# Attention products in a lent bank, k^T v joined to a q run, and where batch 2's k and v are loaded

## The chip, the cores and the metric

The kernel runs on one core of a Trainium2 chip. The metric is the time of one execution on the device, in microseconds (us), as the median of several runs. One further execution is taken with the hardware profiler; its trace gives the start and duration of every instruction. The engines are named as in the profile: PE (TensorE, its weight loads apart as PEld), DVE (VectorE), ACT (ScalarE), POOL (GpSimd) and SP (SyncE, which issues DMAs). POOL and ACT issue DMAs too. PSUM is the memory that PE writes, in eight banks of 512 float32 columns on 128 partitions; ACT and DVE read it.

## The reference

Eight batches of eight heads, 576 rows, head dimension 64. For each head a 64x64 product of k and v, then q times that product, a root-mean-square normalisation, and the result goes, with heads side by side, into a gated feed-forward layer.

```python
kv = np.einsum('bhsd,bhse->bhde', k, v)
out = np.einsum('bhsd,bhde->bhse', q, kv)
rms = np.sqrt(np.mean(out * out, axis=-1, keepdims=True) + 1e-06)
attn = out / rms * g_norm
x = attn.transpose(0, 2, 1, 3).reshape(4608, 512)
gate = 1.0 / (1.0 + np.exp(-(x @ w_gate)))      # 512 -> 1536
val = x @ w_val
result = (gate * val) @ w_out                   # 1536 -> 512
```

All data are float32 (the weights arrive as float64 and are converted on the chip). Batches are counted from 0 here, as in the code.

## The kernel before, in words

**Chunks.** The 4608 rows are nine chunks of 512. Chunk 0 is computed directly: `plain` (matmuls at L599) for the first layer, L833 for the second. Its matmuls are 128x128 by 512 columns. While it runs, DVE and ACT convert the weights in steps (`convert_step`, CV in the list of places), and POOL forms sums of weights (`w1_sums`, steps W0 and W1). Chunks 1 to 8 use a scheme with fewer products and more sums: 26 products for each of three column groups j in the first layer (`PRODUCTS1`, matmuls at L957, 78 places p = 26 j + i) and 26 in the second (`PRODUCTS2`, L1059). What is done with a product's result stands as text behind it: `o5=A` is a copy by ACT (L923), `o1=o1+B` a sum by DVE (L927), `s2` a sigmoid by ACT (L916), `o5*o1` a product by POOL (L919). In chunk 1 sums of weights of the second layer (`w_form`, L1030 and L1032) are made on DVE and POOL at listed places, and stored to DRAM for later chunks.

**Banks.** The products' results lie in five PSUM banks, numbered 0 to 4. `free` is a queue of them: a product that begins a new result takes the oldest free bank, and `give` puts it back at the end once the program has issued its last reader. The remaining three banks are one tile, `at`, for the attention.

**Attention.** Chunk 0's rows all come from batch 0, whose attention is done ahead of it (`attention`, before 33 us) and isn't touched by the change. While chunk c is computed, batch c+1 passes through `feed`; batch 1 passes through during chunk 0, and batch 2 begins there. A batch has two runs m of four heads. Its steps are:

- `load_late(b)`: eight loads of 256 KB of k and v for the first 512 rows (L134, all on SP), and four loads of 64 KB for the other 64 rows (L139, the tile `rest`; on SP for batch 1, on POOL for batch 2, on ACT for later ones). They land in `h_more`, which has other uses between batches.
- `load_q_run(b, m)`: q of four heads, as eight loads of 72 KB in 128-byte pieces (L119) and four of 8 KB, which hold the last 64 columns of two heads a second time (L120). On POOL for batch 1, else on SP.
- `kv_mm`: k^T v of all eight heads, 32 products with 128 rows of contraction (L389), then 8 of 64 rows, the tails (L396), into one `at` tile. Each product writes a 64x64 block.
- `kv_copy`: two ACT copies into `kvq` (L404, L405). The second puts the heads of rows 64 to 127 a second time on rows 0 to 63.
- `turn`: DVE transposes of q into `qTs` (L408, and L410 for the repeated 64 columns).
- `u_mm` (once for each run): q times k^T v, 36 products of 64x64x64 (L439) into an `at` tile. Slots 0 to 15 of the tile are filled by heads g=0 (rows 0 to 63 of `qTs`, bank 0) and g=1 (rows 64 to 127, bank 1) in turn. The last two slots, 16 and 17, both lie in bank 2, and both are computed on rows 0 to 63, the second from the repeated data.
- `u_square` (ACT, L444), sums (DVE, L447), root (ACT, L450), norms (ACT L479, or DVE L455), and `x_turn` (DVE L462, L464, then DMAs on SP).

**Order.** The order on each engine is the program's order, written by hand. For chunk 0 it is the string `places`: a number is the count of plain matmuls issued, and behind it stand the steps put there. KV and C are `kv_mm` and `kv_copy` of batch 1; au to ax1 and bu to bx1 are its runs 0 and 1; LL2 is `load_late(2)`; KV2, ASIDE and D are batch 2's `kv_mm`, a copy of its result to `kv_ahead`, and the later copy from there to `kvq`. Between KV2 and D batch 1 still needs `kvq`. For chunks 1 to 6 it is the string `where` in `feed`: place p of the first layer, and the steps behind it (u0 and u1 are `u_mm` of the two runs, q0 and q1 `u_square`). From chunk 2 on, `kv_mm` and `kv_copy` are put at places 19 and 20 (21 and 22 for batch 3) by the loop at the end of the file. An instruction that waits holds up everything behind it on its engine.

Of the kernel before, what the change touches and what calls it, by code (L numbers as in the profile page):

```python
# [10 lines left out]
FP32 = mybir.dt.float32  # L11
# [9 lines left out]
def kernel(  # L21
# [34 lines left out]
    NRUN = NHP // 2  # L56
    QW = 2 * S + 2 * HD

# [46 lines left out]
    def load_q_run(b, m):  # L105
        if b >= B:
            return
        if b == 1:
            t = h_main[2 - m].rearrange("p s c -> p (s c)")[:, 4 * NT * P - QW:4 * NT * P]
        else:  # L110
            t = sb.tile([P, QW], FP32, tag="q", name="q", bufs=1)
        main = t[:, 0:2 * S].rearrange("p (e j c) -> p e j c", e=2, c=QB)
        more = t[:, 2 * S:QW].rearrange("p (e j c) -> p e j c", e=2, c=QB)
# [11 lines left out]
    def load_late(b):  # L125


        if b >= B:
            return
        mains = {}  # L130
        for n in range(NHP):
            for name, src in (("k", k), ("v", v)):
                mains[n, name] = t = kv_place(len(mains))
                nc.sync.dma_start(out=t.rearrange("p (h c) -> p h c", h=2),  # L134
                                  in_=src[b, 2 * n:2 * n + 2, 0:S4].rearrange("h (p j) d -> p h (j d)", j=NK4))
        rest = kv_place(len(mains))
        for i, src in enumerate((k, v)):
            for r in range(2):
                (nc.sync if b == 1 else nc.gpsimd if b == 2 else nc.scalar).dma_start(out=rest[PH * r:PH * r + PH, GH * i:GH * i + GH].rearrange("p (h d) -> p h d", d=HD),  # L139
                                  in_=src[b, NHP * r:NHP * r + NHP, S4:S].rearrange("h p d -> p h d"))  # L140
        kv_late[b] = mains, rest
# [126 lines left out]

    kvq = const.tile([P, 2, NRUN, 2, HD], FP32, name="kvq")
    kv_ahead = const.tile([P, NRUN, 2, HD], FP32, name="kv_ahead")  # L270
# [19 lines left out]
    def attention(n, at_ps):  # L290

        b, m = divmod(n, NHP)
        d = {}
        kv = kvq[:, 0, m // 2, m % 2]

# [80 lines left out]
    def feed(b):  # L376

        d = {}

        def kv_mm():  # L380

            mains, rest = kv_late[b]
            d["kv"] = ps = at_ps()[:, 0:NRUN, 0:2 * HD].rearrange("p m (e d) -> p m e d", d=HD)
            for m in range(NRUN):
                for e in range(2):
                    for j in range(NK4):
                        for g in range(2):
                            c = slice(NK4 * HD * e + HD * j, NK4 * HD * e + HD * j + HD)
                            nc.tensor.matmul(ps[HD * g:HD * g + HD, m, e], mains[2 * m + g, "k"][:, c],  # L389
                                             mains[2 * m + g, "v"][:, c],  # L390
                                             start=(e == 0 and j == 0), stop=False, skip_group_check=True)
            for e in range(2):
                for m in range(NRUN):
                    for g in range(2):
                        rs, c = slice(PH * m, PH * m + PH), HD * (2 * g + e)
                        nc.tensor.matmul(ps[HD * g:HD * g + HD, m, e], rest[rs, c:c + HD],  # L396
                                         rest[rs, GH + c:GH + c + HD], start=False, stop=True, skip_group_check=True)

        def kv_set_aside():
            nc.scalar.copy(out=kv_ahead, in_=d["kv"])  # L400
            d["kv"] = kv_ahead

        def kv_copy():
            nc.scalar.copy(out=kvq[:, 0], in_=d["kv"])  # L404
            nc.scalar.copy(out=kvq[0:HD, 1], in_=d["kv"][HD:P])  # L405

        def turn(m, e):
            nc.vector.transpose(qTs[:, S * e:S * e + S], q_late[b, m][:, S * e:S * e + S])  # L408
            if e == 1:
                nc.vector.transpose(qTs[0:HD, 2 * S:QW], q_late[b, m][0:HD, 2 * S:QW])  # L410
                if b > 1:
                    load_q_run(b + (m + 1) // NRUN, (m + 1) % NRUN)
                elif m == NRUN - 1:
                    load_q_run(b + 1, 0)

        def heads_run(m):
# [12 lines left out]

            def u_mm():  # L430
                d["u"] = u = at_ps().rearrange("p r c -> p (r c)")[:, 0:2 * S]
                for t in range(NSL + 1):
                    for g in range(2):
                        if t < NSL - 1 or g == 0:
                            head, s_ = (1, NSL - 1) if t == NSL else (g, t)
                            o = HD * place(head, s_)
                            for e in range(2):
                                c = 2 * S + HD * e if t == NSL else S * e + HD * s_
                                nc.tensor.matmul(u[HD * e:HD * e + HD, o:o + HD],  # L439
                                                 qTs[HD * g:HD * g + HD, c:c + HD],  # L440
                                                 kvq[HD * g:HD * g + HD, t == NSL, m, e], start=True, stop=True)

            def u_square():
                nc.scalar.activation(out=sq, in_=d["u"], func=AF.Square)  # L444

# [44 lines left out]

        kv = [kv_mm, kv_copy, kv_set_aside] if b == 2 else [kv_mm, kv_copy]
        t0, t1 = ([lambda m=m, e=e: turn(m, e) for e in range(2)] for m in range(NRUN))
        u0, u1 = heads_run(0), heads_run(1)
        if b == 1:
            return kv, t0 + t1 + u0 + u1, ()
# [4 lines left out]
                   51:x00 52:x01 53:u1 56:q1 57:s10,s11 60:r1 62:n10,n11 63:n12 65:n13 66:n14 68:n15 69:n16""" if b == 2 else """  # L500
                   5:t00 8:t01 28:u0 29:t10 30:q0 33:s00,s01 36:r0 39:t11 41:n00 47:n01 51:x00,x01 54:u1
                   56:q1,s10,s11 61:r1 64:n10 66:n11""" if b == 3 else """
                   3:t00 7:t01 28:u0,t10 30:q0,s00,s01 37:r0 39:t11 47:n00,n01 53:x00,x01 54:u1
                   56:q1,s10,s11 60:r1 61:n10 63:n11"""
# [63 lines left out]
    def at_ps():  # L568
        return psum.tile([P, NAT, 512], FP32, tag="at", name="at")
# [212 lines left out]
    def w1_form(c, j, part, v):  # L782
        if c == 1:
# [12 lines left out]
    batch1, second_batch = feed(1), feed(2)  # L796
    named = {"LL": lambda: load_late(1), "LL2": lambda: load_late(2), "KV": batch1[0][0], "KV2": second_batch[0][0],
             "W0": lambda: w1_sums(0), "W1": lambda: w1_sums(1),
             "ASIDE": second_batch[0][2], "CV": convert_step}
    named.update({"C": batch1[0][1], "D": second_batch[0][1]})  # L800
    for i in range(NRUN):
        named[f"Q{i}"] = lambda i=i: load_q_run(1, i)
        named.update({f"t{i}{e}": batch1[1][2 * i + e] for e in range(2)})
    for i, which in enumerate("ab"):
        for n, step in enumerate(("u", "sq", "s0", "s1", "rt", "rc", "n0", "n1", "n2", "x0", "x1")):
# [326 lines left out]
    for c in range(1, NG):  # L1132
# [4 lines left out]
        if c + 1 < B:  # L1137
            kv, first_, then = second_batch if c == 1 else feed(c + 1)
            for p, step in (list(zip((21, 22) if c == 2 else (19, 20), kv)) if c > 1 else []) + first_:
                at1.setdefault(p, []).append(step)  # L1140
# [9 lines left out]
        if c == 1:  # L1150
            for at_, forms in ((at1, ((28, 9, 0), (30, 10, 0), (34, 12, 0), (52, 11, 1), (53, 22, 0), (57, 14, 0), (58, 8, 1), (61, 19, 0), (64, 16, 1))), (at2, ((1, 13, 0), (3, 23, 0), (4, 25, 1), (9, 15, 0), (10, 24, 0), (10, 20, 0), (11, 17, 0), (12, 18, 0), (13, 21, 0)))):
                for p, n, pool_ in forms:
# [35 lines left out]
```

## Time and profile before

| what | value |
|---|---|
| median of 3 runs | 1002.54 us (1002.2 to 1002.74) |
| the profiled execution | 1003.68 us |
| its span, first to last instruction | 1001.9 us |
| granted PE clock | 1.0 throughout |
| PE busy with ordinary products of the first layer of chunks 1 to 8, L957 | 51% of the chain |
| the second layer of these, L1059 | 27% of the chain |
| plain matmuls of chunk 0, L599 and L833 | 12% of the chain |
| q times k^T v, L439, 14 runs | 2% of the chain |
| k^T v, L389, 7 batches | 1% of the chain |

The span is what lies between the first and the last recorded instruction; the rest of an execution's time lies around it. The chain is the row of work that ended last, followed back from the last instruction: at each step to what released it, or to the instruction before it on its engine. A matmul of the source is two PE instructions in the trace (float32), and its weights are loaded by two PEld instructions. A duration of a matmul is that of one result passing through, longer than the distance between two starts; a run's time is read from the chain, where pieces follow each other.

In the timelines a row is: start in us, length in us, engine, line, operation, output from input, shapes, how many, and in brackets the idle time of that engine before it, with what ended it.

### The profile page before, as it was taken

How to read it: one execution, taken by the hardware profiler on the slowest of the kernel's cores; microseconds unless marked ns; L12 is line 12 of the kernel's file. 1: busy time of each engine (PE TensorE's matmuls, PEld its weight loads, DVE VectorE, ACT ScalarE, POOL GpSimd, SP SyncE). 2: the span in 40 equal slices, each digit the busy share in tenths (PEclk: the TensorE clock that was granted, in tenths of full speed). 3: DMA queues.
4: the chain of work that ended last, by engine and by line, in shares of the span. 5: the costliest groups of instructions: out<-in, count | busy, mean ns of one | idle time of the engine just before them, and what ended most of it. 6: DMA issues, size and time to landing. Idle time of an engine off the chain costs nothing.

```text
span 1001.9 us, 16623 instructions
## 1 busy us (share of the span) xinstructions
PE 993.2 (99%) x5958; PEld 815.9 (81%) x5958; DVE 723.3 (72%) x1199; ACT 342.2 (34%) x606; POOL 617.8 (62%) x991
## 2 busy tenths in 40 slices
PE   8999999999999999999999999999999999999998
PEld 7445447888888888888888888888888888888887
DVE  4889999889757756784677576866587566755672
ACT  4566322652144213530344124421442133213320
POOL 1509997798259633965196708861596349744963
PEclk9999999999999999999999999999999999999999
DMA  9996514764899568746975677756754555444614
GB/s 256 285 263 192 173 42 119 220 220 134 271 294 267 176 183 239 240 158 197 278 220 170 186 218 244 196 171 193 235 198 159 161 176 208 157 148 162 216 50 124
DMA packets 155155, 195.43 MB, mean 195 GB/s; under 512 B 83809, under 2 KB 127841, under 8 KB 155073
## 3 DMA queue, kind: packets, MB, share of 16 engines
q0 software_dynamic: 22128, 114.37, 34.4%
q1 hardware_dynamic: 126864, 78.16, 27.9%
q10 hardware_dynamic: 6080, 1.84, 0.8%
q8 instruction: 47, 0.77, 0.3%
q14 instruction: 36, 0.29, 0.1%
HBM read 160.50 MB, written 25.56 MB: 186 GB/s over the span
## 4 chain that ended last, share of the span: by engine, by line
PE 94%; POOL 2%; DMA 1%; ACT 1%; SPq 1%; issue 1%; DVE 1%; POOLq 0%; ACTq 0%; DVEq 0%
PE mm L957 51%; PE mm L1059 27%; PE mm L599 8%; PE mm L833 4%; PE at L439 2%; PE at L389 1%; DMA v<-in_v_dram 1%; PE at L599 1%; POOL h_more L733 1%; POOL h L733 1%; POOL h L919 0%; POOL w L1030 0%; SPq L93 0%; PE at L396 0%; DVE sg L927 0%
## 5 line engine op out<-in xcount | busy, mean ns | idle before, releaser
L957 PE MATMUL mm<-xs,w 128*128 128x256 f32 x1428 | 331.9, 380 | 0.0
L957 PEld LDWEIGHTS mm<-xs,w 128*128 128x128 f32 x1428 | 270.4, 190 | 37.4 <-DVE sg L927 0.4
L957 PE MATMUL mm<-xT,w 128*128 128x256 f32 x948 | 229.8, 380 | 0.0
L957 PEld LDWEIGHTS mm<-xT,w 128*128 128x128 f32 x948 | 179.5, 190 | 25.0 <-issue 0.2
L780 POOL DMA_DIRECT2D w<-kept x84 | 46.7, 556 | 192.5 <-PE mm L957 188.5
L927 DVE TENSOR_TENSOR sg<-sg,mm 128x512 f32<-128x512 f32 (+1 forms) x176 | 100.8, 600 | 85.0 <-PE mm L957 40.3
L1059 PE MATMUL mm<-w,h 128*128 128x256 f32 x630 | 142.8, 379 | 0.0
L1059 PEld LDWEIGHTS mm<-w,h 128*128 128x128 f32 x630 | 119.7, 190 | 16.3
L919 POOL TENSOR_TENSOR h<-h,sg 128x512 f32<-128x512 f32 x72 | 96.7, 1360 | 56.4 <-DVE h L927 30.4
L923 ACT COPY temps<-mm 128x512 f32<-128x512 f32 (+1 forms) x128 | 66.1, 538 | 186.7 <-PE mm L1059 94.7
L733 POOL TENSOR_TENSOR h<-h 128x128 f32<-128x128 f32 x216 | 113.1, 535 | 16.5 <-DVE h_more L733 13.1
L1059 PE MATMUL mm<-w,h_more 128*128 128x256 f32 x474 | 108.2, 379 | 0.0
L916 ACT ACTIVATE sg<-sg 128x512 f32<-128x512 f32 x96 | 59.7, 630 | 133.6 <-DVE sg L927 133.6
L1059 PEld LDWEIGHTS mm<-w,h_more 128*128 128x128 f32 x474 | 90.1, 190 | 12.2
L923 ACT COPY sg<-mm 128x512 f32<-128x512 f32 (+1 forms) x112 | 56.9, 510 | 86.4 <-PE mm L1059 45.0
L733 POOL TENSOR_TENSOR h_more<-h 128x128 f32<-128x128 f32 x120 | 61.6, 517 | 35.0 <-DVE h L919 30.8
L927 DVE TENSOR_TENSOR temps<-temps,mm 128x512 f32<-128x512 f32 (+1 forms) x96 | 59.4, 619 | 25.7 <-PE mm L1059 16.5
L599 PE MATMUL mm<-xT,w 128*128 128x512 f32 x176 | 77.8, 596 | 0.1
L927 DVE TENSOR_TENSOR temps<-mm,temps 128x512 f32<-128x512 f32 (+1 forms) x64 | 39.8, 622 | 50.7 <-PE mm L1059 24.3
L923 ACT COPY h<-mm 128x512 f32<-128x512 f32 x48 | 28.1, 585 | 138.3 <-PE mm L957 138.3
L927 DVE TENSOR_TENSOR sg<-mm,sg 128x512 f32<-128x512 f32 (+1 forms) x64 | 39.7, 620 | 46.7 <-PE mm L957 24.7
L599 PEld LDWEIGHTS mm<-xT,w 128*128 128x128 f32 x176 | 32.6, 190 | 39.2 <-issue 36.1
(148 smaller groups left out, 1283.6 us busy)
## 6 DMA issues: line engine op xcount, KB each, us to landing
w<-kept POOLq DMA_DIRECT2D x42, 896.0 KB, 5.4
w<-kept POOLq DMA_DIRECT2D x90, 384.0 KB, 4.8
w<-kept POOLq DMA_DIRECT2D x42, 768.0 KB, 5.0
out_dram<-sg SPq DMA_DIRECT2D x119, 64.0 KB, 1.7
h_more<-in_k_dram SPq DMA_DIRECT2D x28, 256.0 KB, 5.5
h_more<-in_v_dram SPq DMA_DIRECT2D x28, 256.0 KB, 6.2
q<-in_q_dram SPq DMA_DIRECT2D x96, 72.0 KB, 5.0
xT<-xTs SPq DMA_DIRECT2D x96, 72.0 KB, 4.6
```

The costliest lines, as they stand in the source:

```text
L389: nc.tensor.matmul(ps[HD * g:HD * g + HD, m, e], mains[2 * m + g, "k"][:, c], mains[2 * m + g, "v"][:, c], start=(e == 0 and j == 0), stop ...
L439: nc.tensor.matmul(u[HD * e:HD * e + HD, o:o + HD], qTs[HD * g:HD * g + HD, c:c + HD], kvq[HD * g:HD * g + HD, t == NSL, m, e], start=True ...
L599: nc.tensor.matmul(self.ps[i], w[("wg", "wv")[i], self.f][:, m, :], xT[self.c][:, m, :], start=(m == 0), stop=(m == NMT - 1), skip_group_c ...
L733: ops.append((eng, lambda v=v, x=x, sign=sign, y=y, eng=eng: eng.tensor_tensor(out=h_form(v, j), in0=h_form(x, j), in1=h_form(y, j), op=op ...
L780: nc.gpsimd.dma_start(out=granule(g)[:, 0:n], in_=kept1[g // NPA % N3, g % NPA][:, 0:n])
L833: nc.tensor.matmul(ps[t], gv[0, f][:, P * t:P * t + P], w["wo", f], start=(f == 0), stop=(f == NFT - 1), skip_group_check=True)
L916: nc.scalar.activation(out=o["o" + step[1]], in_=o["o" + step[1]], func=AF.Sigmoid)
L919: mult.tensor_tensor(out=o[x], in0=o[x], in1=o[y], op=ALU.mult)
L923: nc.scalar.copy(out=o[out_], in_=o[expr])
L927: tt(out=o[out_], in0=o[x], in1=o[y], op=ALU.add if sign == "+" else ALU.subtract)
L957: nc.tensor.matmul(regions[name][1][:, g], ws[:, g], xf[c][wv], start=(new and g == 0), stop=True, skip_group_check=True)
L1059: nc.tensor.matmul(regions[name][1], h_form(hv, j), ws[:, j], start=(used[i] and j == 0), stop=(j == N3 - 1), skip_group_check=True)
```

## The change

Five things are changed.

1. `u_mm` takes a second bank, `lent`: bank 4 for batch 1, else the oldest free one. Slot 17 (the last one of heads g=1) is computed on rows 64 to 127 into the first 64 columns of that bank. `u_square` begins with an ACT copy of these 64 columns into the `at` tile and, past batch 1, gives the bank back. So the repeated columns of q (their loads and their transpose) and the second half of `kvq` go.
2. `kv_mm` is no longer a step by itself. For batch 1 and for batches 3 to 7 it is issued at the start of `u_mm` of the batch's own run 0, right behind it `kv_copy`, then the q products. For batch 2 it is issued at the start of `u_mm` of batch 1's run 1. Its results lie in two banks: run 0's in the `at` tile, run 1's in the lent bank. The tails come first, except in batch 2.
3. `kv_copy` and `kv_set_aside` are two copies of 128 columns, one for each run.
4. The eight 256 KB loads of batch 2's k and v are issued by POOL instead of SP.
5. Places: batch 1's k^T v goes from 20 to 29 (in au), batch 2's stays at 44 with bu, which was at 47; bsq goes from 48 to 47, ASIDE from 44 to 47. In batches 3 to 7 u0 goes from place 28 to 25. In chunk 1 the sum for form 14 of w_out (DVE) goes from place 57 to 55.

```diff
-    QW = 2 * S + 2 * HD
+    QW = 2 * S
...
-                queue.dma_start(out=more[QB * i:QB * i + QB, e], in_=src[:, JR - 2:JR])
...
-                nc.sync.dma_start(out=t.rearrange("p (h c) -> p h c", h=2),
+                (nc.gpsimd if b == 2 else nc.sync).dma_start(out=t.rearrange("p (h c) -> p h c", h=2),
...
-        def kv_mm():
+        def kv_mm(at, lent):
             mains, rest = kv_late[b]
-            d["kv"] = ps = at_ps()[:, 0:NRUN, 0:2 * HD].rearrange("p m (e d) -> p m e d", d=HD)
+            d["kv"] = ps = [t.rearrange("p (e d) -> p e d", d=HD)
+                            for t in (at[:, NAT - 1, 2 * HD:4 * HD], lent[:, HD:3 * HD])]
+            def tails(first):
+                for e in range(2):
+                    for m in range(NRUN):
+                        for g in range(2):
+                            rs, c = slice(PH * m, PH * m + PH), HD * (2 * g + e)
+                            nc.tensor.matmul(ps[m][HD * g:HD * g + HD, e], rest[rs, c:c + HD],
+                                             rest[rs, GH + c:GH + c + HD], start=first and e == 0, stop=not first,
+                                             skip_group_check=True)
+            if b != 2:
+                tails(True)
             for m in range(NRUN):
                 for e in range(2):
                     for j in range(NK4):
                         for g in range(2):
                             c = slice(NK4 * HD * e + HD * j, NK4 * HD * e + HD * j + HD)
...
+                            nc.tensor.matmul(ps[m][HD * g:HD * g + HD, e], mains[2 * m + g, "k"][:, c],
+                                             mains[2 * m + g, "v"][:, c], start=(b == 2 and e == 0 and j == 0),
+                                             stop=(b != 2 and j == NK4 - 1), skip_group_check=True)
+            if b == 2:
+                tails(False)
         def kv_copy():
-            nc.scalar.copy(out=kvq[:, 0], in_=d["kv"])
-            nc.scalar.copy(out=kvq[0:HD, 1], in_=d["kv"][HD:P])
+            for m in range(NRUN):
+                nc.scalar.copy(out=kvq[:, m], in_=d["kv"][m])
...
-                nc.vector.transpose(qTs[0:HD, 2 * S:QW], q_late[b, m][0:HD, 2 * S:QW])
...
-            def u_mm():
-                d["u"] = u = at_ps().rearrange("p r c -> p (r c)")[:, 0:2 * S]
-                for t in range(NSL + 1):
+            def u_mm(first=()):
+                at = at_ps()
+                d["u"] = u = at.rearrange("p r c -> p (r c)")[:, 0:2 * S]
+                i_ = 4 if b == 1 else free.popleft()
+                lent = bank(i_)
+                for step in first:
+                    step(at, lent)
+                for s_ in range(NSL):
                     for g in range(2):
...
+                        o = HD * place(g, s_)
+                        to = lent[:, 0:HD] if s_ == NSL - 1 and g == 1 else u[:, o:o + HD]
+                        for e in range(2):
+                            c = S * e + HD * s_
+                            nc.tensor.matmul(to[HD * e:HD * e + HD], qTs[HD * g:HD * g + HD, c:c + HD],
+                                             kvq[HD * g:HD * g + HD, m, e], start=True, stop=True)
+                d["lent"] = i_, lent[:, 0:HD], u[:, o:o + HD]
             def u_square():
+                i_, lent, to = d["lent"]
+                nc.scalar.copy(out=to, in_=lent)
+                if b > 1:
+                    give(i_)
                 nc.scalar.activation(out=sq, in_=d["u"], func=AF.Square)
...
+        if b == 2:
+            kv = [kv_mm, kv_copy, kv_set_aside]
+        else:
+            u0[0] = lambda u_mm=u0[0]: u_mm((kv_mm, lambda at, lent: kv_copy()))
+            kv = []
...
+    named["bu"] = lambda: batch1[1][2 * NRUN + 11]((second_batch[0][0],))
...
-        18:CV,CV 19:t01 20:KV 22:CV,CV,C 25:CV 26:CV,CV 29:au,LL2 30:CV
+        18:CV,CV 19:t01 22:CV,CV 25:CV 26:CV,CV 29:au,LL2 30:CV
...
-        43:ax1 44:KV2,ASIDE 46:CV,W0 47:bu 48:CV,CV,bsq 50:CV,bs0 52:CV,CV 54:bs1 55:CV,CV,brt,D 57:CV,CV 58:CV 60:CV,brc
+        43:ax1 44:bu 46:CV,W0 47:bsq,ASIDE 48:CV,CV 50:CV,bs0 52:CV,CV 54:bs1 55:CV,CV,brt,D 57:CV,CV 58:CV 60:CV,brc
```

More of the change, by code (lines that the diff above doesn't have):

```diff
@@ L111, in load_q_run @@
             t = sb.tile([P, QW], FP32, tag="q", name="q", bufs=1)
-        main = t[:, 0:2 * S].rearrange("p (e j c) -> p e j c", e=2, c=QB)
-        more = t[:, 2 * S:QW].rearrange("p (e j c) -> p e j c", e=2, c=QB)
+        main = t.rearrange("p (e j c) -> p e j c", e=2, c=QB)
         queue = nc.gpsimd if b == 1 else nc.sync
@@ L266 @@
     g_col = const.tile([P, 1], FP32, name="g_col")
-    kvq = const.tile([P, 2, NRUN, 2, HD], FP32, name="kvq")
+    kvq = const.tile([P, NRUN, 2, HD], FP32, name="kvq")
     kv_ahead = const.tile([P, NRUN, 2, HD], FP32, name="kv_ahead")
@@ L293, in attention @@
         d = {}
-        kv = kvq[:, 0, m // 2, m % 2]
+        kv = kvq[:, m // 2, m % 2]
         def kv_mm():
@@ L388, in kv_mm @@
                             c = slice(NK4 * HD * e + HD * j, NK4 * HD * e + HD * j + HD)
[L389 to L397, printed above, removed]
+                            nc.tensor.matmul(ps[m][HD * g:HD * g + HD, e], mains[2 * m + g, "k"][:, c],
[3 more added lines that the diff above has]
+                tails(False)
         def kv_set_aside():
-            nc.scalar.copy(out=kv_ahead, in_=d["kv"])
-            d["kv"] = kv_ahead
+            for m in range(NRUN):
+                nc.scalar.copy(out=kv_ahead[:, m], in_=d["kv"][m])
+            d["kv"] = [kv_ahead[:, m] for m in range(NRUN)]
         def kv_copy():
-            nc.scalar.copy(out=kvq[:, 0], in_=d["kv"])
-            nc.scalar.copy(out=kvq[0:HD, 1], in_=d["kv"][HD:P])
+            for m in range(NRUN):
+                nc.scalar.copy(out=kvq[:, m], in_=d["kv"][m])
         def turn(m, e):
@@ L428, in by_head @@
                 return t.rearrange("p (n d) -> p n d", d=HD)
-            def u_mm():
-                d["u"] = u = at_ps().rearrange("p r c -> p (r c)")[:, 0:2 * S]
-                for t in range(NSL + 1):
-                    for g in range(2):
[L434 to L441, printed above, removed]
+            def u_mm(first=()):
[6 more added lines that the diff above has]
+                for s_ in range(NSL):
+                    for g in range(2):
+                        o = HD * place(g, s_)
[5 more added lines that the diff above has]
+                d["lent"] = i_, lent[:, 0:HD], u[:, o:o + HD]
             def u_square():
+                i_, lent, to = d["lent"]
+                nc.scalar.copy(out=to, in_=lent)
+                if b > 1:
+                    give(i_)
                 nc.scalar.activation(out=sq, in_=d["u"], func=AF.Square)
@@ L489, in heads_run @@
                     [lambda i=i: x_turn(i) for i in range(NC)])
-        kv = [kv_mm, kv_copy, kv_set_aside] if b == 2 else [kv_mm, kv_copy]
         t0, t1 = ([lambda m=m, e=e: turn(m, e) for e in range(2)] for m in range(NRUN))
         u0, u1 = heads_run(0), heads_run(1)
+        if b == 2:
[3 more added lines that the diff above has]
+            kv = []
         if b == 1:
@@ L500, in feed @@
                    51:x00 52:x01 53:u1 56:q1 57:s10,s11 60:r1 62:n10,n11 63:n12 65:n13 66:n14 68:n15 69:n16""" if b == 2 else """
-                   5:t00 8:t01 28:u0 29:t10 30:q0 33:s00,s01 36:r0 39:t11 41:n00 47:n01 51:x00,x01 54:u1
+                   5:t00 8:t01 25:u0 29:t10 30:q0 33:s00,s01 36:r0 39:t11 41:n00 47:n01 51:x00,x01 54:u1
                    56:q1,s10,s11 61:r1 64:n10 66:n11""" if b == 3 else """
-                   3:t00 7:t01 28:u0,t10 30:q0,s00,s01 37:r0 39:t11 47:n00,n01 53:x00,x01 54:u1
+                   3:t00 7:t01 25:u0 28:t10 30:q0,s00,s01 37:r0 39:t11 47:n00,n01 53:x00,x01 54:u1
                    56:q1,s10,s11 60:r1 61:n10 63:n11"""
@@ L796 @@
     batch1, second_batch = feed(1), feed(2)
-    named = {"LL": lambda: load_late(1), "LL2": lambda: load_late(2), "KV": batch1[0][0], "KV2": second_batch[0][0],
+    named = {"LL": lambda: load_late(1), "LL2": lambda: load_late(2),
              "W0": lambda: w1_sums(0), "W1": lambda: w1_sums(1),
              "ASIDE": second_batch[0][2], "CV": convert_step}
-    named.update({"C": batch1[0][1], "D": second_batch[0][1]})
+    named["bu"] = lambda: batch1[1][2 * NRUN + 11]((second_batch[0][0],))
+    named.update({"D": second_batch[0][1]})
     for i in range(NRUN):
@@ L804 @@
     for i, which in enumerate("ab"):
-        for n, step in enumerate(("u", "sq", "s0", "s1", "rt", "rc", "n0", "n1", "n2", "x0", "x1")):
+        for n, step in list(enumerate(("u", "sq", "s0", "s1", "rt", "rc", "n0", "n1", "n2", "x0", "x1")))[which == "b":]:
             named[which + step] = batch1[1][2 * NRUN + 11 * i + n]
@@ L1138 @@
             kv, first_, then = second_batch if c == 1 else feed(c + 1)
-            for p, step in (list(zip((21, 22) if c == 2 else (19, 20), kv)) if c > 1 else []) + first_:
+            for p, step in first_:
                 at1.setdefault(p, []).append(step)
@@ L1150 @@
         if c == 1:
-            for at_, forms in ((at1, ((28, 9, 0), (30, 10, 0), (34, 12, 0), (52, 11, 1), (53, 22, 0), (57, 14, 0), (58, 8, 1), (61, 19, 0), (64, 16, 1))), (at2, ((1, 13, 0), (3, 23, 0), (4, 25, 1), (9, 15, 0), (10, 24, 0), (10, 20, 0), (11, 17, 0), (12, 18, 0), (13, 21, 0)))):
+            for at_, forms in ((at1, ((28, 9, 0), (30, 10, 0), (34, 12, 0), (52, 11, 1), (53, 22, 0), (55, 14, 0), (58, 8, 1), (61, 19, 0), (64, 16, 1))), (at2, ((1, 13, 0), (3, 23, 0), (4, 25, 1), (9, 15, 0), (10, 24, 0), (10, 20, 0), (11, 17, 0), (12, 18, 0), (13, 21, 0)))):
                 for p, n, pool_ in forms:
```

## The prediction

> **What bounds the kernel now.** I read the page's busy shares and its chain first, then the chain in order of time, then the timelines around the attention steps.
>
> ```profile
> PE 993.2 (99%) x5958; PEld 815.9 (81%) x5958; DVE 723.3 (72%) x1199; ACT 342.2 (34%) x606; POOL 617.8 (62%) x991
> PE 94%; POOL 2%; DMA 1%; ACT 1%; SPq 1%; issue 1%; DVE 1%; POOLq 0%; ACTq 0%; DVEq 0%
> ...
> 475.84 17.27 PE mm L957 x80
> 493.10 2.02 PE at L389 x64
> 495.12 0.39 PE at L396 x16
> 495.51 7.97 PE mm L957 x36
> 503.48 1.31 PE at L439 x72
> 504.79 22.64 PE mm L957 x104
> ```
>
> TensorE is the bound: from 33 us on the chain is one unbroken row of its work, so only TensorE time counts. The last six rows (start, us) are batch 4: k^T v is 64+16 instructions (each product of the source is two), then nine ordinary products, then q times k^T v, 72 instructions. 17.27/80 is 0.216 us an ordinary instruction; 36 of them should take 7.77 but take 7.97. **So a stretch between two small runs costs 0.20 more**: single starts show 0.09 on going into a small run and 0.10 at the first ordinary instruction after it.
>
> Weight loads of one q run (stretches of 0.23 us; third figure PE busy, fourth PEld):
>
> ```profile
> 503.87:504.10 0.23, 0.23 (x29) 0.23 (x24) 1.00 0.00 0
> 504.10:504.33 0.23, 0.23 (x29) 0.23 (x24) 1.00 0.00 0
> 504.33:504.56 0.23, 0.23 (x23) 0.23 (x16) 1.00 0.00 0
> ```
>
> Full stretches touch 24 weight loads, the last one 16. The single starts say why: 64 instructions go in fours, one four each 0.058 us, the last eight in twos at the same pitch. Those are the slots of the last 64 columns, both done on rows 0 to 63.
>
> **What the change does to that path.**
> (A) The last slot of heads g=1 goes to rows 64 to 127 and a lent bank, so the last eight instructions go as two fours, not four twos: 2 x 0.058 = 0.117 us a run, 14 runs: -1.64. Bounds: 0 (fours don't form) to 1.64. I take 1.64: the 64 others already go in fours, with the two row halves in different banks, which the lent bank keeps.
> (B) k^T v moves next to a q run in all seven batches, and one stretch between small runs goes: 7 x 0.20 = 1.4. For batch 2 k^T v ends with the 64-row tails and q follows in the same shape; the 0.09 of a shape change may go too. Bounds 1.4 to 1.5; I take 1.4, the row of the stretch alone. The row behind the rest is L389 to L396, 0.152 between starts where 0.058 is the pitch. The Trainium skill, TensorEngine Tiling (Array Packing), Key Properties, says that changing the tiling mode drains TensorE and changing the tile does not; by it the 0.09 goes in batch 2 and stays in the other six, and (B) would be 1.5. No run shows the tail-to-q step yet.
> (C) A joined q run needs the copies of its own k^T v. They are now one of 128 columns for each run, and the first q product needs the first copy alone. ACT in batch 4:
>
> ```profile
> 495.58 0.37 ACT L404 COPY kvq<-at 128x256 f32<-128x256 f32 x1 [0.94 <-PE at L396]
> ...
> 499.92 0.63 ACT L916 ACTIVATE sg<-sg 128x512 f32<-128x512 f32 x1 [1.96 <-DVE sg L927]
> 501.79 0.58 ACT L923 COPY h<-mm 128x512 f32<-128x512 f32 x1 [1.23 <-PE mm L957]
> ```
>
> The copy starts 0.07 after its matmul and takes between 0.22 (64 columns, L479) and 0.37 (256): about 0.45 to the release. Meanwhile TensorE does run 1's 32 instructions, 64 in 2.02, so 1.0 us. ACT is free: its sigmoid of product 23 ended at 500.55 and product 25 at 500.8. Cost 0; without the cover 0.45 a batch, 2.7 over six. The lent slot waits for the second copy, but 0.93 us of q products stand ahead of it. Tails first costs nothing: the shape changes are as many.
> (D) Lent banks. In batch 1 bank 4 is idle. Later the run takes the oldest free bank, and the next products get banks whose readers are one step younger. The tightest row is batch 7: DVE's last read of the bank (`h<-mm,temps`, 740.62 for 0.68) ends at 741.30; the lent write comes 0.93 after the run's start at 740.88. Margin 0.5; cost 0, at worst 0.3 in that one batch.
> (E) The 14 new ACT copies of 64 columns (0.22 to 0.37) stand ahead of the Square. For most the next user is half a microsecond or more away. Not in the second run of batch 2: there the copy `sg<-mm` behind the Square ends at about 210.5, and TensorE goes onto that bank at 210.83 without waiting. A copy of 0.25 to 0.37 more: 0 to 0.2; I take +0.1.
> (F) The sum for form 14 of w_out goes from place 57 to 55, on DVE:
>
> ```profile
> 210.09 1.41 DVE L447 TENSOR_REDUCE ms<-sqs 128x9 f32<-128x576 f32 x2 [1.28 <-ACT sqs L444]
> 211.42 1.95 DVE L1032 SCALAR_TENSOR_TENSOR w<-w,w 128x768 f32<-128x768 f32 x1
> ...
> 224.91 2.68 DVE L927 TENSOR_TENSOR sg<-sg,mm 128x512 f32<-128x512 f32 x4
> 226.94 1.10 PE L957 MATMUL mm<-xs,w_ring 128*128 128x256 f32 x4 [0.41 <-POOL h L733]
> ```
>
> DVE stood idle 1.28 us ahead of the reduce, then did the sum, and ran late until TensorE stopped at 226.94. The page names POOL, but that product goes onto a bank that DVE's third `sg<-sg,mm` reads until about 226.8. The row costs 0.65 (the four instructions ahead started at 225.50: 0.57; a slow restart 0.08). In the new order the sum fills the idle time. Part of the lateness comes back from ACT's copies and from DVE's 2.29 us `sg<-temps` at 222.51. Between 0.65 gained and 0.3 lost; I take -0.35.
> (G) Batch 2's eight k, v loads leave SP for POOL and now wait for batch 1's k^T v, at place 29 instead of 20:
>
> ```profile
> 53.66 1.25 POOL L139 DMA_DIRECT2D h_more<-in_k_dram  x2 [12.24 <-PE at L396]
> ...
> 76.37 0.74 POOL L751 TENSOR_TENSOR h_more<-w 128x256 f32<-128x256 f32 x1 [20.24 <-PE at L389]
> ```
>
> Run 0 of batch 1's k^T v will end near 60.05 (the q run began at 61.22, less 2.4 for k^T v now ahead of it in the same place, plus 0.5 tails and 1.0). POOL is idle there. Eight issues of 0.62 end at 65.1, and landing takes 5.9 (median of L134): 71. The four small ones wait for the first landing and land near 73. k^T v of batch 2 starts at 75.3 and needs run 0's loads then, run 1's a microsecond later, the small ones at 77.3. Cost 0. POOL's w1 sums stand behind these loads but start only at 76.37, after that k^T v, as before. On SP nothing gains: the loads behind the old ones started at 61.37, when DVE freed their buffer. Worst rows: an issue takes 1.19 (q load at 37.75, beside DVE's TENSOR_SCALAR), a landing 9.3: 60.05+8x1.19+9.3 = 78.9, 2.8 late. Bounds 0 to 2.8.
> (H) Costs nothing: ASIDE after q on ACT (it lets DVE's 1.40 idle us at 79.60 go; TensorE wasn't waiting there), 14 transposes of 0.26 and 56 loads of 8 KB fewer, q of batches 3 to 7 three places sooner.
>
> Sum: -1.64 - 1.4 + 0.1 - 0.35 = **-3.3 us**: span 1001.9 to 998.6. The profiled execution was 1003.68, 1.8 around its span; the runs' median 1002.54 is 1.1 below it. Off the median: **999.2 us**.
>
> **Rivals.**
> R1, slower: the POOL loads come late. Place: k^T v of batch 2. With x us an issue, 60.05+8x+5.9 must stay under 76.3 for run 1: it costs from x = 1.3 with a median landing, from 0.9 with the longest. To undo 3.3 and add 2 the loads must be 5.3 late: x of 1.96. For: 0.62 became 1.19 beside TENSOR_SCALAR. Against: the 84 issues of L780 take 0.53 to 0.59, and most of DVE's work at 60 to 66 is of kinds beside which the four issues at 53.66 took 0.62. Time 1004.5 or more. The Trainium skill, SBUF — State Buffer, A bandwidth-pool intuition that's wrong, tells of a POOL-issued DMA of 620 ns that takes 3100 beside a DVE copy; that would be 60+25+6 = 91, a stop of over 14 us, about 1014. The trace agrees in kind (1.05 and 1.19 beside TENSOR_SCALAR) and not in size.
> R2, no change: joined runs wait for ACT. If the first copy isn't back under run 1's products, 0.45 x 6 = 2.7 comes back: 1001.9. For: ACT is in order, and a sigmoid waiting for DVE stands ahead. Against: (C).
> R3, it doesn't do what it says: no fours in the last slot. Then -1.7: 1000.9. Against: (A).
> R4, DVE's lateness stays or grows in batch 2's stage: 0 to +0.5 instead of -0.35: 999.6 to 1000.1, still faster.
>
> **How the numbers follow.** Under 0.2%, 2.0 us, counts as no change, about what this measurement can tell. Forecast with R4: 0.76. R2, R3 and a part of R1's wait (1000.6 to 1004.5): 0.16. R1 in full: 0.08. Faster 0.76, same 0.16, slower 0.08. The likeliest case alone spans 998.2 (all of F, nothing of E) to 1000.2; the range goes from 998.0 to 1001.8, with R3 and most of R2 in it.
>
> **What would show it.** (A) a q run of 1.19 us, not 1.31. (B) no small k^T v run by itself in the chain, and k^T v with q about 3.6 us. (C) no idle TensorE before the first q product. (E) one gap near 210, (F) a smaller one at 226. (G) no gap at 75; a wait for DMA there is R1. Wrong would be a new gap at the start or the end of each joined run, or a bank waiting for DVE in every batch.

## The result, and the profile after

The changed kernel takes 1000.61 us (median of 13 runs, 999.24 to 1002.56) and the kernel before 1003.45 us in the same rounds (13 runs, 1002.20 to 1005.34): a ratio of 0.9969, 95% interval [0.9959, 0.9978]. The forecast was 3.3 us less; measured are 2.8. The profiled execution took 1001.39 us, its span 999.6, against 1003.68 and 1001.9.

The page of the changed kernel (busy shares), its chain by engine, and three stretches of the chain in order of time (start, us, what): VectorE in chunk 0, batch 2's second run, and batch 4.

```profile
PE 992.4 (99%) x5958; PEld 816.2 (82%) x5958; DVE 719.1 (72%) x1185; ACT 343.0 (34%) x621; POOL 616.2 (62%) x991
...
PE 93%; DVE 4%; issue 1%; ACT 1%; DMA 0%; SPq 0%; DVEq 0%; ACTq 0%
...
128.69 1.64 DVE w L235
130.37 27.73 PE mm L853 x64
...
206.13 1.14 PE at L450 x66
207.28 0.04 PE at L450 x2
207.34 21.02 PE mm L977 x96
...
497.54 1.08 PE at L400 x32
498.62 0.93 PE mm L400 x32
499.55 1.14 PE at L450 x66
500.70 0.04 PE at L450 x2
500.76 25.34 PE mm L977 x116
```

TensorE is still the bound. k^T v (L400, behind its tails L389) and q times k^T v (L450) now stand next to each other, and the nine ordinary products that were between them are gone. One thing is new: in chunk 0's second layer the chain goes through VectorE, which still converts w_out (L235) when TensorE wants it.

To see where the 2.3 us of this pair of executions came from, I compared the start of the same ordinary TensorE instruction in both, one after another to the end. The difference moves only at these places:

| Where | us, after minus before |
|---|---|
| before the first late batch (start-up) | +0.45 |
| (A) 14 q runs, each 1.209 and not 1.311 | -1.44 |
| (B) joins: six of -0.197, batch 2's -0.355 | -1.54 |
| (F) stop at 226.94 gone | -0.645 |
| a stop of 0.26 in batch 7 (738.59 before) gone | -0.26 |
| new: two stops in chunk 0's second layer (122.64, 129.64) | +0.53 |
| new: six starts that come 0.104 late (210.83, 293.31, 399.64, 505.98, 612.32, 718.65) | +0.62 |
| sum | -2.28 |

So the change is worth 2.73 us behind the start-up, and two new costs take back 1.15 of what it gave. The late starts come about here (ScalarE's timeline in batch 3, then TensorE's weight loads: start, us, line, what; in brackets the idle time before it and what ended it):

```profile
290.92 0.59 ACT L943 COPY h<-mm 128x512 f32<-128x512 f32 x1 [1.14 <-PE mm L977]
291.40 0.22 ACT L456 COPY at<-mm 128x64 f32<-128x64 f32 x1
291.65 1.13 ACT L459 ACTIVATE sqs<-at 128x1152 f32<-128x1152 f32 x1
292.68 1.07 ACT L943 COPY sg<-mm 128x512 f32<-128x512 f32 x2
```

```profile
293.31 0.73 PEld L977 LDWEIGHTS mm<-xs,w 128*128 128x128 f32 x4 [0.24 <-ACT sg L943]
```

The q run ended at 288.02, but its Square starts at 291.65: it was issued behind the copy `h<-mm`, which waits for a product until 290.92. The next copy, `sg<-mm`, frees the bank of product region B (a name in the kernel's table of products) at about 293.2, and TensorE writes there again at 293.31. The margin is 0.05 us. The weight loads around it start 0.216 apart, one product ahead; this one waits for that copy and starts only at 293.31, together with its own product. That product's result takes 0.104 us more to pass, and every start behind it comes 0.104 late. The records of the products show no idle time for it; only those of the weight loads do.

### The profile page after: what moved, and what is told of

Read it like the earlier page. It is cut to its first block, busy times and chain, and to the rows that moved or that the text cites. A ratio compares the mean times of both kernels' runs of the same rounds, so it can differ in the third digit from the quotient of the medians.

```text
span 999.6 us, 16578 instructions
## 1 busy us (share of the span) xinstructions
PE 992.4 (99%) x5958; PEld 816.2 (82%) x5958; DVE 719.1 (72%) x1185; ACT 343.0 (34%) x621; POOL 616.2 (62%) x991
## 4 chain that ended last, share of the span: by engine, by line
PE 93%; DVE 4%; issue 1%; ACT 1%; DMA 0%; SPq 0%; DVEq 0%; ACTq 0%
PE mm L977 54%; PE mm L1079 27%; PE mm L618 5%; PE mm L853 3%; PE at L450 2%; DVE cz L226 1%; DVE w L222 1%; DVE w L195 1%; PE at L400 1%; PE mm L400 1%; DVE cz L210 0%; DMA q<-in_q_dram 0%; PE two L326 0%; DVE w L235 0%; DVE h L626 0%
## 5 line engine op out<-in xcount | busy, mean ns | idle before, releaser
L752 POOL TENSOR_TENSOR h<-h 128x128 f32<-128x128 f32 x216 | 109.9, 521 | 16.6 <-DVE h_more L752 13.1
L752 POOL TENSOR_TENSOR h_more<-h 128x128 f32<-128x128 f32 x120 | 58.5, 491 | 34.8 <-DVE h L939 30.5
```

The lines of the kernel that those rows point to most:

```text
L752: ops.append((eng, lambda v=v, x=x, sign=sign, y=y, eng=eng: eng.tensor_tensor(out=h_form(v, j), in0=h_form(x, j), in1=h_form(y, j), op=op ...
```

## The experiments

Each kernel is the changed kernel with the edit shown; differences are start to start, against the changed kernel's first profile, without the start-up before the first late batch (59 us, 51 in experiment 7; on that, see the last section). Experiments 1 to 7 are one execution each. Rows of places are cut to what changes; where several rows get the same edit (batch 3 has its own row), one is shown.

**1. The Square later.** Batch 2's second run likewise, 56 to 57.

```diff
-28:t10 30:q0,s00,s01 37:r0
+28:t10 31:q0,s00,s01 37:r0
```

> Batches 3 to 7 issue the first run's slot copy and Square at place 31 instead of 30, batch 2 its second run's at 57 instead of 56, so that on ScalarE they stand behind the copy of product bank B (and of A) and not ahead of it. Theory (ScalarE's order): the six starts of TensorE that come 0.10 us late (210.83, 293.31, 399.64, 505.98, 612.32, 718.65 in the changed kernel's trace) go, because the copy ends about 1.3 us sooner; TensorE's work from the first batch to the end shrinks by 6 x 0.104 = 0.6 us, or by 0.5 if one bank comes late elsewhere. Rival (the joined run itself or the turn of the banks makes them late): at least five of the six stay, or as many turn up within two products of the old places; the change is within 0.15 us.

The six late starts went, each 0.104, as the theory had it. But TensorE now stopped once in each of the six batches, 0.60 us in batches 3 to 7 (net +0.49) and 0.74 in batch 2, where VectorE's late reads at 226 cost 0.38 more; in all 3.47 us were lost. The waits of TensorE, then its timeline and ScalarE's in batch 3:

```profile
PE mm L977 <- ACT temps L943: 2.1, 6, 0.5
```

```profile
291.99 0.22 ACT L456 COPY at<-mm 128x64 f32<-128x64 f32 x1
292.24 1.13 ACT L459 ACTIVATE sqs<-at 128x1152 f32<-128x1152 f32 x1
293.27 1.07 ACT L943 COPY temps<-mm 128x512 f32<-128x512 f32 x2
```

```profile
294.39 1.13 PE L977 MATMUL mm<-xT,w 128*128 128x256 f32 x4 [0.33 <-ACT temps L943]
```

The cause of the late starts is shown: which copy stands behind the Square is the one that comes late. Moving it behind bank B's copy made the next one, `temps<-mm`, late, and by more. Neither theory had named that.

**2. The joined run later.**

```diff
-25:u0 28:t10 30:q0,s00,s01 37:r0
+28:u0,t10 30:q0,s00,s01 37:r0
```

> In batches 3 to 7 the joined run goes back from place 25 to 28, its Square stays at 30. Theory (ScalarE's order): the Square then starts as soon as the run ends, and the deadline of bank B's copy moves three products less far from it, so the five late starts near 293, 400, 506, 612 and 719 go (0.5 us), and the one at 210.83, which is in batch 2 and not touched, stays. Rival (the length of the joined run is what makes the copy late): they stay, because 3.6 us of a run stand between the copies wherever it is put; the change is within 0.15 us.

Neither. At place 28 k^T v reads k and v after the sums of h have been written over them (their places lie in h_more, and those sums start at place 26). So it multiplies overwritten data, and it waits for GpSimd's sums. The waits of TensorE:

```profile
PE at L400 <- POOL h_more L752: 16.5, 9, 3.0
```

The run took 1027.60 us. It says nothing on the late starts; it shows that a run with k^T v in it can't stand at place 28 and had to go ahead of place 26, which brings bank B's deadline nearer to the Square.

**3. Batch 1's second run with batch 2's k^T v at place 47.**

```diff
-43:ax1 44:bu 46:CV,W0 47:bsq,ASIDE 48:CV,CV 50:CV,bs0
+43:ax1 46:CV 47:bu,W0 48:bsq,ASIDE,CV,CV 50:CV,bs0
```

> Batch 1's second run with batch 2's k^T v goes from place 44 to 47, behind the end of the ordinary block it cuts, and its Square from 47 to 48, behind the block's gate. Theory (VectorE's late conversions): VectorE's 1.77 us of idle time at 80.4 us shrinks to under 0.4, its conversions of w_out come 1.3 to 1.8 us sooner, and TensorE's two stops at 122.64 and 129.64 (0.53 us with their slow restarts) go; the time falls by 0.4 to 0.5 us. Rival 1 (the conversions are bounded by VectorE's whole load, or by the arrival of the staged words, not by this idle stretch): idle time turns up elsewhere before 120 us and the stops keep at least 0.4 us. Rival 2: GpSimd's sums of w1, which start 1.3 us later with it, make TensorE wait after 140 us, and nothing is gained.

Both stops went: -0.534 us between 116 and 158 us, and no other place moved. VectorE's timeline around place 47, first of the changed kernel, then of this one:

```profile
78.63 1.75 DVE L226 SCALAR_TENSOR_TENSOR cz<-st,cz 128x1024 uint32<-128x1024 uint32 x1
82.14 0.69 DVE L626 TENSOR_TENSOR h<-mm,sg 128x512 f32<-128x512 f32 x1 [1.77 <-PE mm L618]
82.75 1.35 DVE L233 SCALAR_TENSOR_TENSOR w<-w,g_col,cz 128x1024 f32<-128x1024 f32 x1
...
121.84 1.21 DVE L235 TENSOR_TENSOR w<-w,cz 128x1024 f32<-128x1024 f32 x1
```

```profile
78.36 1.23 DVE L226 SCALAR_TENSOR_TENSOR cz<-st,cz 128x1024 uint32<-128x1024 uint32 x1
79.50 0.68 DVE L626 TENSOR_TENSOR h<-mm,sg 128x512 f32<-128x512 f32 x1
80.10 1.27 DVE L233 SCALAR_TENSOR_TENSOR w<-w,g_col,cz 128x1024 f32<-128x1024 f32 x1
83.51 0.76 DVE L462 TENSOR_REDUCE ms<-sqs 128x9 f32<-128x576 f32 x1 [2.13 <-ACT sqs L459]
...
121.26 1.21 DVE L235 TENSOR_TENSOR w<-w,cz 128x1024 f32<-128x1024 f32 x1
```

At place 44 the joined run, 3.46 us, stands in the middle of an ordinary block; the block's end and its gate come later by that much, VectorE's multiply waits for them, and the conversions queue behind it. At 47 the multiply starts 2.6 us sooner, with no idle time before it. Most of that is lost again: VectorE now idles 2.13 us for the Square, which is later too, and its conversion of w_out at 121 comes 0.58 us sooner and not 1.3 to 1.8. The stops, 0.33 us without their slow restarts, needed no more. So rival 1 was right that idle time turns up elsewhere and wrong that the stops stay. Rival 2 fell as well: GpSimd's sums of w1 made nobody wait.

**4. The sum for form 14 back.**

```diff
-(53, 22, 0), (55, 14, 0),
+(53, 22, 0), (57, 14, 0),
```

> The sum for form 14 of w_out goes back from place 55 to 57, all else as in the changed kernel. Theory (it was this move that took the stop at 226.94 away): VectorE idles again ahead of the sums of squares near 209, is late at 225, and TensorE stops near 226 for 0.55 to 0.75 us. Rival (the lent bank and the new turn of the banks took the stop away, and the move did nothing): no stop over 0.1 us near 226, the time within 0.15 us of the changed kernel's.

The stop came back: +0.63 us near 226 (0.556 of stop and 0.075 of a slow restart). VectorE's timeline in this kernel, then TensorE's:

```profile
209.59 1.41 DVE L462 TENSOR_REDUCE ms<-sqs 128x9 f32<-128x576 f32 x2 [1.42 <-ACT sqs L459]
210.92 1.79 DVE L1052 SCALAR_TENSOR_TENSOR w<-w,w 128x768 f32<-128x768 f32 x1
...
224.26 2.67 DVE L947 TENSOR_TENSOR sg<-sg,mm 128x512 f32<-128x512 f32 x4
```

```profile
226.29 1.10 PE L977 MATMUL mm<-xs,w_ring 128*128 128x256 f32 x4 [0.39 <-POOL h L752]
```

VectorE idles 1.42 us ahead of the reduce again and reaches the four reads of the banks at 224.26; in the changed kernel it does the sum in that idle time and reaches them at 223.18. So the rest of the change doesn't take the stop away; the move does. (In chunk 0's second layer this execution lost 0.12 us more, with TensorE 0.9 us earlier out of the start-up than in the changed kernel's profile.)

**5. Batch 2's loads back on SP.**

```diff
-(nc.gpsimd if b == 2 else nc.sync).dma_start(out=t.rearrange("p (h c) -> p h c", h=2),
+nc.sync.dma_start(out=t.rearrange("p (h c) -> p h c", h=2),
```

> Batch 2's eight k, v loads go back to SP's queue, where they now wait for batch 1's joined run (58.2 to 60.0 us) with the loads of the staged weights and of q behind them. Theory (the queue matters: on SP they would hold up what stands behind): the staged load issued at 61.91 and the q loads at 62.32 start 3 to 6 us later, VectorE converts later, and TensorE's stop in chunk 0's second layer, 0.53 us in the changed kernel, grows to between 1 and 4 us. Rival (the queue does not matter, what stands behind them has slack): k^T v of batch 2 starts without a wait, as with GpSimd, the stop stays between 0.4 and 0.7, the time within 0.2 us.

+0.03 us: the rival. On SP the eight issues take 0.37 to 0.47 each and the staged load behind them starts at 62.69; TensorE waits for none of it. This part of the change neither gains nor costs.

**6. Tails last.** In batches 1 and 3 to 7:

```diff
-            if b != 2:
-                tails(True)
...
-            if b == 2:
-                tails(False)
+            tails(False)
```

> In batches 1 and 3 to 7 the 64-row tails of k^T v go behind its 128-row instructions, as batch 2 has them; the copies of k^T v can then start only at the run's last few instructions. Theory (tails first hides the copies): the first q product waits for ScalarE, 0.3 to 0.5 us in each of the six runs, less 0.1 to 0.2 for one change of shape fewer; the time grows by 0.6 to 2.4 us in all. Rival (the copies' cover was not needed): no wait, and the six runs get 0.1 to 0.2 shorter, 0.6 to 1.2 us less in all.

Each of the six runs takes 0.42 us longer, 2.53 in all, a little above the range's upper end. TensorE's timeline in batch 3:

```profile
285.60 0.23 PE L389 MATMUL mm<-h_more 64*64 64x64 f32 x2
286.18 1.21 PE L447 MATMUL at<-kvq,qTs 64*64 64x64 f32 x66 [0.35 <-ACT kvq L410]
```

From the last tail to the first q product pass 0.57 us. Batch 2, whose copies go elsewhere, shows this order without a wait: 3.46 us for the run, against 3.62 with tails first and 4.04 here. The cover that tails first gives is thus worth 0.58 a batch (4.04 less 3.46), less the 0.16 for a change of shape more (3.62 less 3.46).

**7. k^T v by itself again**, with its halves still in a batch's bank and a lent one:

```diff
-            u0[0] = lambda u_mm=u0[0]: u_mm((kv_mm, lambda at, lent: kv_copy()))
-            kv = []
+            def kv_alone():
+                d["i"] = 4 if b == 1 else free.popleft()
+                kv_mm(at_ps(), bank(d["i"]))
...
-        44:bu 46:CV,W0 47:bsq,ASIDE 48:CV,CV 50:CV,bs0
+        44:KV2,ASIDE 46:CV,W0 47:bu 48:CV,CV,bsq 50:CV,bs0
```

> k^T v stands by itself again (batch 1 at place 20, batch 2 at 44 with q at 47, batches 3 to 7 at 19), with its two halves still in a batch's bank and a lent one; the last q slot stays in a lent bank, loads, sums and places otherwise as in the changed kernel. Theory (each join saves one stretch between two small runs): six batches get 0.20 longer and batch 2 0.36, 1.54 us in all; the stop of 0.53 us in chunk 0's second layer shrinks below 0.2, because VectorE's idle 1.77 us at 80.4 goes with the separate places; the time grows by 0.9 to 1.6 us. The late starts near 293 and later stay, since Square and copies keep their order. Rival (q runs in fours, not the join, brought the gain; the changes of shape cost the same apart): within 0.3 us of the changed kernel.

+3.1 us, but 2.14 of it are the edit's own: batch 3's k^T v, at place 19 where the kernel before had 21, waits for its last v (TensorE's timeline):

```profile
280.83 0.33 PE L400 MATMUL mm<-h_more 128*64 128x64 f32 x2
282.64 1.12 PE L400 MATMUL mm<-h_more 128*64 128x64 f32 x30 [1.48 <-DMA h_more<-in_v_dram]
```

The rest is +1.01: 1.54 for the seven stretches that are back, less the 0.53 of the two stops, which are gone. From batch to batch it takes 0.20 us more than the changed kernel, and the late starts are there as expected: they come from the Square's place, not from the join.

**8. Both cures.** The run at 47 as in experiment 3, and the Square a place sooner, in ScalarE's idle time:

```diff
-28:t10 30:q0,s00,s01 37:r0
+28:t10 29:q0 30:s00,s01 37:r0
...
-53:u1 56:q1 57:s10,s11
+53:u1 55:q1 57:s10,s11
```

> The joined run of batches 1 and 2 at place 47, and the Squares sooner: batches 3 to 7 at 29 instead of 30, batch 2's second at 55 instead of 56, so that copy and Square stand in ScalarE's idle 1.14 us (2.55 us in batch 2) ahead of the copy of product bank C. Theory: Square then starts at about 290.0 instead of 291.65, bank B's copy ends 0.9 us sooner than now, all six late starts go and bank C's copy, about 0.2 us later, is still in time: against the changed kernel 0.53 + 6 x 0.104 = 1.16 us less of TensorE's span from 59 us on, about 4.0 us under the kernel before. Rival (whichever copy stands behind the Square comes late, as the temps copies did when the Square went to 31): a stop of 0.1 to 0.5 us in each of the six, nothing gained over the run at place 47 alone, or 0.5 to 2.5 us lost.

-1.17 us: -0.534 in chunk 0, and -0.106 at each of the six places. 998.63 us against 1002.49 for the kernel before, ratio 0.9964 [0.9951, 0.9976]. ScalarE in batch 3:

```profile
287.26 0.22 ACT L456 COPY at<-mm 128x64 f32<-128x64 f32 x1
287.51 1.13 ACT L459 ACTIVATE sqs<-at 128x1152 f32<-128x1152 f32 x1
288.54 0.58 ACT L943 COPY h<-mm 128x512 f32<-128x512 f32 x1
289.01 0.60 ACT L943 COPY sg<-mm 128x512 f32<-128x512 f32 x1
```

TensorE is 2.41 us earlier here than in the changed kernel's profile (start-up and chunk 0 included). With that taken off, the Square starts 1.7 us sooner, the copy `h<-mm` 0.03 later, and bank B's `sg<-mm` 1.3 sooner. From 59 us on no instruction of TensorE now waits; what is left between the runs are changes of shape.

**9 and 10. The changed kernel and kernel 8 side by side.**

> The changed kernel once more, beside the next one on the same chip. Theory (TensorE's time from 59 us on is the same in every execution, the time before it differs by up to 2.2 us between executions): 59 us to the end takes what it took before to within 0.05 us, whatever the start was; the median is 1.2 us above that of the run with join at 47 and Square at 29, and 2 to 3.5 us below the kernel before. Rival (the changed kernel starts later of itself): the first batch's work begins at 58.5 to 59.2 us again, and the distance to the next kernel is 2.5 us or more.

> The join at 47 and the Squares at 29 and 55 once more. Theory: median 1.2 us (0.7 to 1.7) below the changed kernel's and 3.5 to 4.3 below the kernel before. Rival (the gain of 1.17 us read from the trace is lost in what differs between executions): within 0.5 us of the changed kernel.

The changed kernel: 999.62 us (6 runs, 999.09 to 999.95), ratio to the kernel before 0.9970 [0.9958, 0.9982]. Kernel 8: 998.65 (7 runs; one stands at 1003.15, the six others lie between 998.17 and 998.96), 0.9965 [0.9952, 0.9977]. The two differ by 0.97 us, inside the 0.7 to 1.7 that was expected, all but one run of kernel 8 lying below the lowest of the other. In the changed kernel the time from 59 us to the end was the same as in the first profile to 0.02 us, while the work before it was done 2.3 us sooner; the rival, that it starts late of itself, fell.

## Why the prediction was right

The sign and the size held, 2.8 us where 3.3 were forecast, because TensorE bounds the kernel and the two large terms are TensorE's own time. That the sum came as near as it did is in part luck: 0.55 us of gain and 1.05 us of cost that the prediction hadn't counted stand against each other. Step by step:

- **(A)** Right in kind: all slots go in fours. 0.103 a run and not 0.117, so -1.44 for -1.64. The missing 0.014 is at the end of the run: in both kernels the next ordinary instruction starts 0.148 behind the run's last one, and the last of a four starts 0.020 behind its first, the last of a two 0.007.
- **(B)** -1.54 for -1.4. The term left open, 0.09 for a change of shape that goes in batch 2, is there, as 0.16: from its last tail to the first q product pass 0.039 us, where L389 to L396 took 0.152 before, and the second four of q starts 0.049 closer behind the first. The Trainium skill's rule (TensorEngine Tiling (Array Packing), Key Properties) that changing the tiling mode drains TensorE and changing the tile does not gave 1.5, and the trace agrees: in the same shape no stop, and about 0.16 for the whole run.
- **(C)** Right. The cost is 0, and the cover without which it would be 2.7 was shown by experiment 6 to be worth 2.5. One sentence was wrong: "Tails first costs nothing: the shape changes are as many." It has one change more than tails last, 0.16 us a batch; the sum doesn't use it.
- **(D), (G)** Right, at nothing. (G)'s eight issues took 0.72 each and not 0.62, from 60.88 on, and k^T v of batch 2 waited for none. (Its upper bound of 2.8 should be 2.6, 78.9 less 76.3.) Experiment 5 adds what the prediction didn't ask: on SP they would have cost nothing either.
- **(E)** The term that was mis-sized: +0.1, for batch 2's second run alone, where +0.62 came, in six places. The prediction said "for most the next user is half a microsecond or more away". That was true for the old places; the joined run's move from 28 to 25, with the Square left at 30, and the lent slot's copy ahead of it took bank B's margin in batches 3 to 7 from 0.97 to 0.05 us. Of these 0.92 the copy is 0.25 (291.40 to 291.65), the move the rest. In batch 2 the copy alone took the margin from 0.29 to 0.05. As a start with a margin of 0.29 was in time there before, either alone would likely have left batches 3 to 7 in time; no run has one without the other. The prediction named the move and booked it under "nothing" in (H). Experiments 1 and 8 show that the Square's place decides it. The prediction's sign of being wrong, a bank waiting for DVE in every batch, came for six of the seven, with ScalarE in DVE's place.
- **(F)** Right in kind, larger: -0.645, the whole stop, where -0.35 was taken. The lateness that was to come back from ScalarE's copies didn't come. Experiment 4 shows the move as the cause.
- **(H)** Wrong in one point: "ASIDE after q on ACT (it lets DVE's 1.40 idle us at 79.60 go)". The 1.40 us went, but 1.77 us came 2.5 us later, because k^T v and q together cut an ordinary block ahead of its end. VectorE thus gained nothing while TensorE came 0.76 us sooner to the weights that VectorE converts: +0.53 (experiment 3). I had looked only at whether TensorE waits there in the kernel before, where the margin was 0.42 to 0.44 us.
- The stop of 0.26 us in batch 7 that went was not foreseen; in the kernel before, a weight load waited there for VectorE's `sg<-mm,sg`. It stays away in experiment 7 too, so it isn't the join; which of the lent banks, the fours or place 25 took it away was not tried.

Against the forecast of -3.3: (A) gave 0.20 less and (B) 0.14 more, (F) and batch 7 gave 0.55 more, (E) and (H) cost 1.05 more; that makes the -2.73. R1 (loads late on GpSimd), R2 (joined runs wait for ScalarE), R3 (no fours) and R4 (VectorE late at 226) did not come; the slow side of the result lay in costs that none of them named.

## What to carry to other kernels

When TensorE is given back time, list every margin behind it that is smaller than the gain, on engines that gain nothing: here a producer that was 0.4 us ahead became the next stop when 0.76 was given back. When a run is moved, move what evacuates it along, and look at which copy then stands behind it in an in-order queue: here the right place for the long instruction was the engine's idle time, not "after the urgent one". A join that cuts a block delays the block's end by the join's whole length for everyone who waits for it.

## What the runs showed of the hardware

**Start-up.** The same work before 59 us took up to 2.4 us more in one execution than in another. TensorE's timeline of the changed kernel in its first profile, then in its second:

```profile
7.80 1.97 PE L671 MATMUL mm<-ident 128*128 128x128 f32 x8
9.70 1.29 PE L326 MATMUL two<-kvq,qTs 64*64 64x64 f32 x40
```

```profile
6.86 1.08 PE L671 MATMUL mm<-ident 128*128 128x128 f32 x8
7.88 0.81 PE L326 MATMUL two<-kvq,qTs 64*64 64x64 f32 x40
```

The same eight matmuls start every 0.213 us in the first and every 0.111 us in the second: TensorE ran at half its pace until about 11 us in the one and until about 5.5 us in the other. The row of the granted clock doesn't show it; it reads full from the first slice. The Trainium skill (TensorE: Matmul & The Clock Gate, The HAM clock gate (the "warmup" mystery)) describes a clock that is halved until a free-running window has seen enough work, around 4 us into sustained work, give or take 0.5 us from run to run. The halved pitch agrees, and so does the second profile, about 4 us behind its first matmul at 1.37; the first profile, more than 9 us behind it, does not. Of the twelve profiles four have the late moment (the changed kernel's first and experiments 2, 3 and 7). It isn't the whole spread: among the other seven of the changed kernel and its variants the work before 59 us still differs by up to 1.5 us. That is why single executions of these kernels are compared here from 59 us on.

**A late weight load.** Where a bank's release left a margin of 0.05 us, TensorE's next start slipped by 0.104 us, with nothing booked as idle but its weight load's 0.24; with a margin of 0.29 (210.83 in the kernel before) it did not. A stop with idle time cost 0.075 or 0.104 on top of it.
